# Attention's order found anew, with the strided copy of the first pairs' keys and the landings of late transposing DMAs costed from the trace

## The chip, the core and the metric

The kernel runs on one core of one Trainium2 chip. The metric is device microseconds from start to end of one execution, the median of the runs. In the text PE is TensorE, DVE VectorE, ACT ScalarE, POOL GpSimd and SP SyncE.

## What is computed

An attention with two kinds of keys feeds a mixture of experts. Each query sees the keys less than 16 positions away and, beside them, 24 summaries of blocks of 32 positions (maximum of the keys, mean of the values). The result is the input x of a gate with eight Sinkhorn steps and of eight experts:

```python
k_sum = k.reshape(B, H, nb, block, D).max(axis=3)
v_sum = v.reshape(B, H, nb, block, D).mean(axis=3)
mask_l = np.abs(pos[:, None] - pos[None, :]) < window
scores_l = np.where(mask_l, scale * q @ k.T, -1e9)
scores_s = scale * q @ k_sum.T + np.log(block)
a = softmax(concat([scores_l, scores_s]))
x = a @ concat([v, v_sum])              # 4 batches, 8 heads, 768 positions, 64 wide
P = np.exp(x @ w_gate)                  # x is 3072 x 512, 8 experts
for _ in range(8):
    P /= P.sum(1); P /= P.sum(0); P *= N / E
for e in range(8):                      # w1[e] is 512 x 1024, w2[e] 1024 x 512
    out += P[:, e] * (np.maximum(x @ w1[e], 0) @ w2[e])
```

## The kernel before, in words

**Stages.** The attention handles two heads at once, a *pair*; there are 16, four to a batch. While it runs, PE also does the products of expert 0, in pieces of 384 tokens, as soon as the four pairs of a batch have given their x: the hidden products (L227, tile `hps`, four matmuls for each 128 of the 1,024 hidden rows), their relu (L220), the projection (L237, tile `yps`, two times four matmuls for each 128 tokens) and the copy of that into `out_acc` (L223). From about 116 us on the other seven experts follow, with products of their own kind.

**A pair.** Keys, queries and values are loaded by DMAs that POOL issues. Pairs 0 to 3 are turned on PE (`tr`, `tr_qh`, tiles `tkq`) and copied out with a stride; their queries and all that follows are done in two halves of 384 positions (`pair_half`). Pairs 4 to 11 are turned on PE and copied out contiguously, pairs 12 to 15 by a transposing DMA on SP's queue (`tr_dma`, L358 to L361, `kT` and `qT`); these twelve are handled whole (`pair_whole`). Then come

- `key_max` on DVE (L376 to L385): the block maxima of the keys, into `ksT`;
- the block sums of the values: PE (`vs`, L399) and DVE (`Vs` or `Ve`, L405, and for the whole pairs the copy of L411);
- `near_values` (L415 to L423), for whole pairs: four small DMAs on SP that fetch the neighbouring values into `Ve`. The buffer `Ve` comes free with the second value product of an earlier pair (for pair 11 that is pair 9);
- the scores (L389, `sg`), the scores against the summaries (L489, `ss`), their exponentials on ACT (L514 and its like);
- the masks on DVE (L454) and, for whole pairs, the edges (L462 and L466, twice each);
- the value products on PE (L477 for whole pairs; L537 and L552 for halves), the normalization on DVE (L555 to L567, the last step in L566);
- x turned back, by PE (`tx`, L573) and a copy, or for pairs 10 to 14 by a transposing DMA on SP.

The zeros beside the masked scores of the half pairs are written once for each of the buffers `Eh` (`pads`, L632 to L643).

**What sets the order.** Every engine runs its own instructions strictly in order. That order comes from a list scheduler, `Plan` (L37 to L138), which runs while the kernel is built. The work is cut into units, each added with an engine (or two to choose from), a cost in us, the units that it waits for, the PSUM banks that it opens or uses and a priority; `lag` is the time from the unit's end on its engine until its result may be used. The planner takes, again and again, the unit that could start first on some engine, by priority among those within 0.02 us. The planner's times decide the order and nothing else: on the chip each instruction waits on semaphores for what it needs. Two tables shift its choice: `RANK` adds to the priority of a unit (the key `"S0.14"` is the scores, `S`, part 0, of pair 14), and `ON` pins a unit that two engines could do to one of them. Names in the tables: `k`, `q`, `v`, `w1` loads; `tr`, `kT`, `qT` turning keys and queries and its copy; `km` key maximum; `vs`, `Vs` block sums; `S`, `X` scores and exponential; `mk`, `ed` masks and edges; `ss`, `sx` summary scores; `A`, `no` value products and normalization; `xt`, `x` x turned and copied; `cl` pads; `near` the neighbours; `lg`, `lo` the gate's logits. A bank of the kind `m` holds, in turn, hidden products, projections, and turned keys and queries of the first pairs. When nothing is ready early on, PE is given matmuls that compute nothing (`keep_busy`, L611), so as not to stand idle.

The units that the change touches are added in `pair_start`: the transposing DMAs (L722), and the copies of turned keys (L730, by `tr_out`, L368, on ACT or DVE).

Of the kernel before, what the change touches and what calls it, by code (L numbers as in the profile page):

```python
# [141 lines left out]
def kernel(  # L142
# [21 lines left out]
    PB = H // 2  # L164
# [89 lines left out]
    if True:  # L254
# [19 lines left out]
        add = plan.add  # L274
# [417 lines left out]
        U = {}  # L692
# [22 lines left out]
        def pair_start(i, prio):  # L715
# [4 lines left out]
            for z in range(2 if i >= PB else 1):  # L720
                if i >= 12:
                    U["tr", i, z] = U["kT", i, z] = add("SP", 1.25, lambda z=z: tr_dma(i, z),  # L722
                                                        [U["kq"[z], i]] + (war_k, war_q)[z], prio, lag=5.5)
                    continue
                buf = Buffer(tag)
                U["tr", i, z] = add("PE", 0.5 if i < PB else 0.335, lambda z=z: tr(i, z, tag),
                                    [U["kq"[z], i], U["ident"]] + (war_k, war_q)[z]
                                    + [U["tr", i, 0] if z else U.get(("S", i - 1, 1 if i > PB else 0))],
                                    prio, opens=[buf], shape="col" if i < PB else None)
                U["kT", i, z] = add({"ACT": 0.7, "DVE": 0.475},  # L730
                                    0, lambda z=z: tr_out(U["kT", i, z].on, i, z), [U["tr", i, z]], prio,
                                    uses=[buf])
# [201 lines left out]
        for i in range(4):  # L934
# [1097 lines left out]
```

## Time and profile before

| | |
|---|---|
| median of 3 runs | 658.6 us (656.7 to 659.61) |
| profiled execution | 658.27 us, span of the core 656.6 us |
| mean granted PE clock | 0.998 |
| hidden products of expert 0 (L227), 256 matmuls | 49.3 us of PE, 1.6 us idle before, released by DVE (L223) |
| DMA | 77.73 MB, mean 118 GB/s |
| PE's busy tenths in 40 equal slices | 8 in the first, 9 in nearly all others |

The time of an execution stands 1.67 us above its span in the profile: the span goes from the first to the last instruction that the trace holds. Rows of the timeline read: start in us from the span's start, length in us, engine, line and operation, what is written and read, tile shapes, and a count where several instructions in a row are drawn together; in brackets the idle time of that engine just before, and what ended it. Rows of the stretches read: the stretch and its length, busy time and count of PE, its weight loads, DVE, ACT and POOL, then granted clock, busy share of the DMA engines and GB/s. A PE row's length counts until its last matmul's end, which overlaps the next row's start; the distance of starts tells what PE really spent.

### The profile page before, as it was taken

The numbers are of one execution on the slowest core, as the hardware profiler recorded it, in microseconds if no ns is written. First come the engines' busy times: TensorE is split into PE (matmuls) and PEld (weight loads), VectorE is DVE, ScalarE is ACT, GpSimd is POOL, SyncE is SP. The second block draws the span as 40 slices with busy tenths as digits, with TensorE's granted clock in tenths as the row PEclk, the third lists the DMA queues.
The fourth block names the chain that finished last, engine by engine and source line by source line (L and its number), as shares of the span: only waits on it lengthen the run. The fifth ranks groups of instructions, "written<-read, shape, count | busy, mean of one in ns | idle before, by whom it ended". The sixth has DMA issues, their size and how long they took to land.

```text
span 656.6 us, 15064 instructions
## 1 busy us (share of the span) xinstructions
PE 646.6 (98%) x5569; PEld 446.8 (68%) x5569; DVE 537.5 (82%) x1341; ACT 533.8 (81%) x1210; POOL 255.4 (39%) x320
## 2 busy tenths in 40 slices
PE   8999989999999999999999999999999999999996
PEld 4666656555677676777776767767667777676775
DVE  8889986778889988887799769878889679976866
ACT  6788975666995678898998989899989899898871
POOL 9599504123001022434244243424343326623422
PEclk9999999999999999999999999999999999999999
DMA  9999988400645376987989599978988799987857
GB/s 157 187 152 148 145 92 99 70 1 8 138 112 111 116 124 87 116 110 98 162 107 121 79 157 128 106 96 122 153 106 107 96 168 125 144 139 158 129 69 192
DMA packets 147368, 77.73 MB, mean 118 GB/s; under 512 B 112736, under 2 KB 125280, under 8 KB 147296
## 3 DMA queue, kind: packets, MB, share of 16 engines
q0 software_dynamic: 124864, 62.64, 81.8%
q1 hardware_dynamic: 21472, 13.68, 8.3%
q8 instruction: 43, 0.70, 0.5%
q10 hardware_dynamic: 960, 0.48, 0.3%
q14 instruction: 29, 0.24, 0.1%
HBM read 55.59 MB, written 45.09 MB: 153 GB/s over the span
## 4 chain that ended last, share of the span: by engine, by line
PE 93%; DMA 3%; POOL 2%; DVE 1%; issue 0%; DVEq 0%
PE pab L1086 17%; PE pg L1086 17%; PE py L1092 16%; PE px L1092 13%; PE px L1472 8%; PE hps L227 6%; PE yps L237 6%; PE pab L1144 4%; DMA kT<-kst 1%; DMA qst<-in_q_dram 1%; PE sg L389 1%; PE tkq L355 1%; POOL vx L324 1%; PE av L477 1%; PE ss L489 1%; PE vs L399 1%
## 5 line engine op out<-in xcount | busy, mean ns | idle before, releaser
L1092 PEld LDWEIGHTS <-hf 128*128 128x128 f16 x1840 | 177.5, 98 | 50.0
L1384 POOL DMA_DIRECT2D out_dram<-out_acc x68 | 61.5, 928 | 163.1 <-ACT out_acc L1360 87.9
L1092 PE MATMUL py<-w,hf 128*128 128x256 f16 x656 | 94.8, 273 | 0.0
L1030 DVE TENSOR_TENSOR hf<-hf 128x1024 f16<-128x1024 f16 x142 | 93.0, 689 | 0.0
L1381 POOL DMA_DIRECT2D out_dram<-out_acc x68 | 64.7, 965 | 60.9 <-ACT out_acc L1360 41.0
L1036 DVE CUSTOM_DVE_ANT_0 hf<-pg,c 128x512 f16<-128x512 f32 x84 | 57.8, 688 | 21.5 <-ACT c L1210 14.1
L1360 ACT ACTIVATE out_acc<-py,P_sb 128x256 f32<-128x256 f32 x136 | 62.8, 487 | 7.6 <-PE py L1092 4.1
L1086 PEld LDWEIGHTS <-ws 128*128 128x128 f16 x504 | 46.6, 98 | 30.8 <-issue 0.2
L1086 PEld LDWEIGHTS <-w 128*128 128x128 f16 x520 | 50.0, 99 | 24.9 <-issue 0.4
L203 POOL DMA_DIRECT2D w<-in_moe_w_dram x56 | 45.2, 877 | 53.2 <-PE pg L1086 51.5
L1036 DVE CUSTOM_DVE_ANT_0 hf<-pab,c 128x512 f16<-128x512 f32 x84 | 57.8, 688 | 9.8 <-ACT c L1217 5.7
L1092 PE MATMUL px<-ws,hf 128*128 128x256 f16 x400 | 59.8, 273 | 0.0
L1092 PE MATMUL px<-w,hf 128*128 128x256 f16 x400 | 59.0, 273 | 0.0
L218 ACT ACTIVATE hf<-pg 128x512 f16<-128x512 f32 x84 | 50.9, 606 | 9.8 <-PE pg L1086 9.1
L218 ACT ACTIVATE hf<-pab 128x512 f16<-128x512 f32 x84 | 49.7, 612 | 7.8 <-PE pab L1086 5.7
L1210 ACT COPY c<-pab 128x512 f32<-128x512 f32 x84 | 49.8, 593 | 6.7 <-PE pab L1086 3.7
L1033 DVE TENSOR_TENSOR px<-px,out_acc 128x256 f32<-128x256 f32 x64 | 27.4, 428 | 34.0 <-PE px L1472 33.4
L1217 ACT COPY c<-pg 128x512 f32<-128x512 f32 x84 | 49.7, 592 | 6.3 <-PE pg L1086 5.0
L1086 PE MATMUL pab<-xT,w 128*128 128x512 f16 x184 | 54.4, 379 | 0.0
L1202 ACT COPY pg<-pab 128x512 f32<-128x512 f32 x84 | 49.8, 594 | 3.2 <-PE pab L1144 3.0
L227 PE MATMUL hps<-xT,w 128*128 128x384 f16 x256 | 49.3, 326 | 1.6 <-DVE out_acc L223 1.6
L1086 PE MATMUL pg<-xT,w 128*128 128x512 f16 x168 | 50.0, 379 | 0.0
(191 smaller groups left out, 1536.8 us busy)
## 6 DMA issues: line engine op xcount, KB each, us to landing
out_dram<-out_acc POOLq DMA_DIRECT2D x136, 256.0 KB, 5.0
w<-in_moe_w_dram POOLq DMA_DIRECT2D x8, 1024.0 KB, 11.9
w<-in_moe_w_dram POOLq DMA_DIRECT2D x56, 128.0 KB, 4.6
out_dram<-out_acc SPq DMA_DIRECT2D x28, 256.0 KB, 2.3
vx<-in_v_dram POOLq DMA_DIRECT2D x16, 192.0 KB, 6.0
qst<-in_q_dram POOLq DMA_DIRECT2D x31, 96.0 KB, 5.3
kst<-in_k_dram POOLq DMA_DIRECT2D x24, 96.0 KB, 5.4
out_acc<-out_dram SPq DMA_DIRECT2D x8, 256.0 KB, 4.2
```

Of the source, the lines that this page charges most:

```text
L218: nc.scalar.activation(out=out, in_=in_, func=AF.Relu, bias=0.0, scale=1.0)
L227: nc.tensor.matmul(hp[:, 0:n], lhsT=w1s[e][:, dk, 128 * f:128 * (f + 1)], rhs=xT[:, dk, t0:t0 + n], start=(dk == 0), stop=(dk == KD - 1))
L1030: nc.vector.tensor_tensor(out=out, in0=in0, in1=in1, op=ALU.subtract)
L1036: nc.vector._custom_dve(TENSOR_ADD_SAT, out=out, in0=in0, in1=in1, s0=FLT_MAX, s1=0.0)
L1086: nc.tensor.matmul(bank[:], lhsT=w[:, dk, :], rhs=x[:, dk, :], start=start and dk == 0, stop=dk == KH - 1, skip_group_check=True)
L1092: nc.tensor.matmul(bank, lhsT=a(f)[:, 128 * c:128 * (c + 1)], rhs=w[:, f, :], start=start and f == 0, stop=f == FH - 1, skip_group_check=True)
L1202: nc.scalar.copy(out=B["g" + K][:], in_=B["a" + K][:])
L1210: nc.scalar.copy(out=B["c5" + K][:], in_=B["b" + K][:])
L1360: nc.scalar.activation(out=out_acc[:, (c, HT + c)[t == tb], k * DH:(k + 1) * DH], in_=at(src), func=AF.Copy, scale=scale[:, t, e:e + 1])
L1381: nc.gpsimd.dma_start(out=rows(ta), in_=out_acc[:, c, :], accum_op=ALU.add)
L1384: nc.gpsimd.dma_start(out=rows(tb), in_=out_acc[:, HT + c, :], accum_op=ALU.add)
L1472: nc.tensor.matmul(half(b, k)[:, g, :], lhsT=still2(e, j, g, w, c)[:, i, :], rhs=moving2a(e, g, v)[:, i, :], start=start and g == 0 and i ...
```

## The change

Three costs that the planner is told, and the two tables. The copy of turned keys of pairs 0 to 3 on DVE, which writes with a stride, costs 0.92 us instead of 0.475; a transposing DMA costs SP 1.4 us instead of 1.25; and its result is taken to land 7.5 us after that instead of 5.5, except for pair 15, where it stays 5.5. `RANK` and `ON` are replaced as a whole by tables found for these costs. No instruction is written differently; which engine does a copy, and the order on each engine, follow from the tables and the costs.

```diff
@@ pair_start @@
                 if i >= 12:
-                    U["tr", i, z] = U["kT", i, z] = add("SP", 1.25, lambda z=z: tr_dma(i, z),
-                                                        [U["kq"[z], i]] + (war_k, war_q)[z], prio, lag=5.5)
+                    U["tr", i, z] = U["kT", i, z] = add("SP", 1.4, lambda z=z: tr_dma(i, z),
+                                                        [U["kq"[z], i]] + (war_k, war_q)[z], prio, lag=5.5 if i == 15 else 7.5)
...
-                U["kT", i, z] = add({"ACT": 0.7, "DVE": 0.475},
+                U["kT", i, z] = add({"ACT": 0.7, "DVE": 0.475 if i >= PB else 0.92},
...
         RANK = {
-            "k": -0.92, "k.0": 8.65, "q0": -9.07, "v.0": -5.38, "k.1": -5.25, "q0.1": -4.8, "k.2": 0.79, "q0.2": -0.22, "k.3": 3.33,
...
+            "k": -0.57, "k.0": -5.54, "q0": 6.25, "v": 1.35, "v.0": -0.65, "k.1": 2.88, "q0.2": 6.38, "v.2": 0.34, "v.3": -1.02,
...
         ON = {
-            "q0.0": "DVE", "cl.1": "DVE", "kT0.0": "DVE", "x0.0": "ACT", "qT0.1": "ACT", "x0.1": "ACT", "kT0.2": "ACT", "qT0.2": "ACT",
-            "x0.2": "ACT", "kT1.0": "ACT", "x1.0": "ACT", "kT1.1": "ACT", "x1.1": "DVE", "kT1.2": "DVE", "kT1.3": "ACT", "x1.3": "DVE",
-            "kT0.4": "ACT", "x.4": "DVE", "kT0.5": "ACT", "kT1.5": "ACT", "kT0.6": "ACT", "x.6": "ACT", "kT0.7": "DVE", "kT1.7": "ACT",
-            "x.7": "DVE", "kT0.8": "ACT", "x.8": "ACT", "kT1.9": "DVE", "kT1.11": "ACT", "x.15": "DVE",
+            "cl.1": "ACT", "x0.0": "ACT", "x0.1": "ACT", "kT0.2": "ACT", "qT0.3": "ACT", "x0.3": "ACT", "x1.0": "DVE", "kT1.1": "DVE",
+            "kT1.2": "ACT", "x1.2": "DVE", "kT0.4": "ACT", "kT1.4": "DVE", "x.4": "ACT", "kT0.5": "DVE", "kT1.5": "ACT", "x.5": "ACT",
+            "kT0.6": "ACT", "kT1.6": "DVE", "x.6": "DVE", "kT0.7": "DVE", "x.7": "ACT", "kT1.8": "DVE", "kT0.9": "ACT", "kT0.10": "DVE",
+            "kT1.10": "ACT", "kT0.11": "ACT", "x.15": "ACT",
         }
```

What the changed tables give, read off the built instruction orders: on PE 11,114 rows (matmuls and weight loads) instead of 11,116, one idle matmul of 19 left out, and the last 8,185 in one order in both programs; DVE 1,251 instructions instead of 1,259, ACT 1,129 instead of 1,132, with the last 886 and the last 968 in the same order; POOL's order unchanged. Engines change for some copies: the pads of the second `Eh` buffer go from DVE to ACT, ahead of the copy of pair 0's first queries; two strided key copies go from DVE to ACT, while DVE gets more of the contiguous copies; three relus of expert 0 go from DVE to ACT. The scores of the last pairs stood on PE in the order 11, 12, 13, 14, 15 and stand as 12, 11, 14, 13, 15. On SP, of the DMAs for the late pairs (`near` is four of them):

```
before: kT12 near10 qT12 kT13 qT13 kT14 near11 qT14 near12 x10 kT15 qT15
after:  kT12 qT12 near10 kT13 qT13 near11 kT14 qT14 near12 x10 kT15 qT15
```

On DVE, the order around pair 14's key maximum becomes: normalization of pair 10, a copy of yps, masks of pair 12, block sums of pair 12, edges of pair 12, first mask of pair 11, key maximum of pair 14, second mask and edges of pair 11, key maximum of pair 13, normalization of pair 11.

90 rows, old and new, of the table RANK are left out of this document.

## The prediction

> **What bounds the kernel now.** I read the page first, for the share of each engine, then the stretches, to see where PE is not full.
>
> ```profile
> span 656.6 us, 15064 instructions
> PE 646.6 (98%) x5569; PEld 446.8 (68%) x5569; DVE 537.5 (82%) x1341; ACT 533.8 (81%) x1210; POOL 255.4 (39%) x320
> ...
> PE 93%; DMA 3%; POOL 2%; DVE 1%; issue 0%; DVEq 0%
> ```
>
> PE has 93% of the chain that ended last: only time in which PE waits, or does matmuls that compute nothing, can be won. The stretches (span, then busy time of PE first) place it.
>
> ```profile
> 82.00:92.00 10.00, 8.42 (x91) 5.18 (x90) 7.61 (x24) 6.94 (x15) 0.35 (x2) 1.00 1.33 124
> ...
> 300.00:400.00 100.00, 100.00 (x837) 71.89 (x836) 80.63 (x174) 89.50 (x220) 38.71 (x46) 1.00 0.91 124
> ```
>
> The expert stage at 300 us has no idle PE, and the last 8,185 of PE's 11,114 rows stand in one order in both programs: that stage only starts earlier or later. The attention stage, 0 to about 116 us, decides. Busy time flatters it, since a pipelined matmul counts until its end, so I read starts. Here is PE in the worst stretch (start, length, and in brackets its idle time).
>
> ```profile
> 83.53 0.81 PE L227 MATMUL hps<-xT,w 128*128 128x384 f16 x4
> 85.91 0.81 PE L227 MATMUL hps<-xT,w 128*128 128x384 f16 x4 [1.57 <-DVE out_acc L223]
> ...
> 86.74 2.28 PE L227 MATMUL hps<-xT,w 128*128 128x384 f16 x12
> 88.86 0.35 PE L477 MATMUL av<-vx,em 128*128 128x65 bf16 x6
> ...
> 89.57 0.32 PE L489 MATMUL ss<-qT,ksT 128*128 128x384 bf16 x1
> 89.73 1.46 PE L227 MATMUL hps<-xT,w 128*128 128x384 f16 x8
> 91.13 0.59 PE L389 MATMUL sg<-qT,kT 64*128 64x160 bf16 x12
> ```
>
> Eight hidden matmuls of L227 take 1.46 us, four 0.81: 0.162 apiece and 0.16 for the last one's end. Four should thus hand over after 0.65, but the next four start 2.38 after them: 1.73 lost. The twelve at 86.74 need 1.94 and hold PE for 2.12: 0.18 more. Together 1.9 us. DVE names the cause.
>
> ```profile
> 81.25 0.56 DVE L566 TENSOR_TENSOR xs<-av,rc 128x384 f16<-128x384 f32 x1
> 84.00 0.36 DVE L381 TENSOR_TENSOR kh<-kT 128x384 bf16<-128x384 bf16 x1 [2.19 <-DMA kT<-kst]
> ...
> 85.18 0.68 DVE L223 COPY out_acc<-yps 128x512 f32<-128x512 f32 x1
> 85.78 0.55 DVE L454 TENSOR_TENSOR em<-er,band 128x768 bf16<-128x768 bf16 x1
> 86.24 0.28 DVE L405 TENSOR_TENSOR Ve<-vs,own 64x128 bf16<-64x128 f32 x1
> ...
> 86.97 0.54 DVE L220 TENSOR_SCALAR h<-hps 128x384 f16<-128x384 f32 x1
> ...
> 87.98 0.19 DVE L462 TENSOR_TENSOR Ee<-er,band 32x80 bf16<-32x80 bf16 x1
> ...
> 88.85 1.03 DVE L454 TENSOR_TENSOR em<-er,band 128x768 bf16<-128x768 bf16 x2
> ```
>
> The key maximum of pair 14 stood at DVE's head, waited 2.19 us for its transposing DMA, and the copy of yps behind it freed PE's bank late. SP's rows of that stretch:
>
> ```profile
> 74.61 2.00 SPq L360 DMA_TRANSPOSE kT<-kst  x1
> 76.72 0.59 SPq L420 DMA_DIRECT2D Ve<-vx  x1
> ...
> 79.41 1.27 SPq L360 DMA_TRANSPOSE qT<-qst  x1
> ```
>
> From issue to landing, the transposing DMAs of L360 as the view of that line has it, and the small copies into Ve as the DMA view has it (number, KB, median):
>
> ```profile
> DMA to landing us min/median/max: 2.7/8.3/9.4
> ```
>
> ```profile
> Ve<-vx SPq DMA_DIRECT2D x48, 10.2 KB, 4.6
> ```
>
> A planner that gives the transposing ones 6.75 us (1.25 and a lag of 5.5), where the median is 8.3, makes that mistake.
>
> **The change part by part.** The three costs are read by the planner alone; what runs differs by order and by engine of evacuation. POOL's queue keeps its order, so the loads stay; PE drops one idle matmul of 19.
>
> *The stretch at 83 us, won.* In the new order the copy of yps follows pair 10's normalization on DVE directly, and pair 14's key maximum stands behind that copy (0.60), both masks of pair 12 (1.03), its block sums (0.73), its edges (0.87) and one mask of pair 11 (0.46): 3.7 us of DVE work after 81.8, so about 85.5. The PE wait of 1.9 us goes: **minus 1.9**. Nothing excludes less; if pair 14's keys came 2 us later still, the masks and edges of pair 11 would wait behind them and the gain would be spent.
>
> *The first 34 us, lost.* Rows first:
>
> ```profile
> 4.69 1.31 ACT L643 COPY Eh<-zeros 128x224 bf16<-128x224 bf16 x3
> 6.08 0.48 ACT L223 COPY qT<-tkq 128x384 bf16<-128x384 bf16 x1
> 9.56 0.94 DVE L223 COPY kT<-tkq 128x768 bf16<-128x768 bf16 x1
> 19.56 0.36 PE L339 MATMUL tkq<-ident,qst 128*64 128x128 bf16 x6 [0.31 <-DMA qst<-in_q_dram]
> 21.43 0.55 DVE L223 COPY qT<-tkq 128x384 bf16<-128x384 bf16 x1
> 22.38 1.01 ACT L514 ACTIVATE erh<-sg 128x992 bf16<-128x992 f32 x1
> 24.65 0.65 PE L537 MATMUL av<-vx,Eh 128*128 128x65 bf16 x16
> 26.55 0.65 PE L537 MATMUL av<-vx,Eh 128*128 128x65 bf16 x16
> 33.03 1.03 PE L237 MATMUL yps<-w,h 128*128 128x512 f16 x4
> ...
> 34.16 0.59 PE L389 MATMUL sg<-qT,kT 64*128 64x160 bf16 x12
> 34.68 0.34 PE L573 MATMUL tx<-ident,xs 128*128 128x128 f16 x3
> ```
>
> The pads of Eh1 move from DVE to ACT and stand ahead of pair 0's query copy: 1.31 us more there, a copy at 7.3 instead of 6.08, first scores 0.7 late. Two strided key copies (0.94 each) leave DVE in return. Both orders then meet at 19.56, where PE waits for a query load that POOL issues as before: until there the change costs **nothing**; the cover is this wait, and without it the 0.7 would count.
>
> From there I count along the new order. Pair 0's second scores now precede pair 1's query copy on DVE (0.55, done at 22.0); on ACT the exponential (1.01) and a query copy precede the fourth x, which frees the first hidden matmuls at about 23.3. Seven hidden matmuls, a score group (0.4) and five more bring the first value product of the second half to 25.7, against 24.65. The new order has by then done that score group, which the old one does later. On to pair 4's scores: four value products (2.6, from rows 24.65 and 26.55 with what lies between), 20 hidden matmuls (3.25), four groups of transposes of x, two of k and q, scores and summaries, about 2.2: 33.75. The old order reaches them at 34.16 with four more yps matmuls (0.87 to the next start) and a summary (0.16) done, 1.03 in all, and one transpose group (0.17) open: like for like 33.3. **Plus 0.45**; bounds minus 0.3 (the score group hidden) and plus 1.2 (what the first exponentials slip).
>
> *The new wait.* Pair 14's scores now stand ahead of pair 13's on PE. PE would reach them at 91.13 (pair 13's scores now), plus 0.52 for pair 14's own, minus 2.63 for what comes between (0.52; 88.86 to 89.57, 0.71; 89.73 to 91.13, 1.40), minus 1.9, plus 0.45: 87.6. Their queries come by the DMA issued at 79.41. On SP the four copies for pair 11 (from 76.72, 2.7 us with all four) move ahead of pair 14's keys; pair 9's second value product, whose end they need, is done some 1.6 us earlier, so I put the copies at 74.0, the keys at 76.5 instead of 74.61, and the queries at 78.4. With 8.3 to 9.4 they land at 86.7 to 87.8; if the engines, not the issue, set the landing, at the old 87.7 to 88.8. PE waits 0 to 1.2, and everything behind it on PE too, since no row passes the head. I take **plus 0.4**, the middle of the nearer half. The keys, at 84.8 to 85.9, meet DVE at 85.5; its 2.5 us up to pair 11's edges end at 88.0 to 88.4, beside the same PE wait.
>
> [...]
>
> Sum: minus 1.9, plus 0.45, plus 0.4 is **minus 1.05**. On the profiled execution, 658.27 us with a span of 656.6, that is a span of 655.5 and a time of 657.2. The median of the three runs is 658.6, 0.3 above, and they spread from 656.7 to 659.6; I put **657.3**.
>
> **The rivals.** *Slower: PE blocks on pair 14's queries.* If the copies for pair 11 go out only at 76.72, as now, keys follow at 79.4, queries at 81.4, and with 9.4 they land at 90.8: a wait of 3.2, a sum of plus 1.8, 660.1. It decides from a landing at 89.0 on. For it: the in-order PE and the issue of 2.00 at 74.61, where SP itself was held. Against: those copies are free to start earlier. *Everything won:* the queries are in time and the first 34 us cost nothing, with 0.3 won there: minus 2.2 and up to 0.25 of smaller waits, 655.9. For it: landings no longer underpriced. *The fix doesn't hold:* keys late, the wait moves from the copy of yps to pair 11's edges; minus 1.9 becomes nothing, sum 0 to plus 0.9: 658.7. For it: the keys are issued 1.9 us later than now.
>
> **How the numbers follow.** Forecast 0.46, everything won 0.22, doesn't hold 0.14, slower 0.18: the new wait sits where a landing that no row shows meets an engine that lets nothing pass, so its bad side weighs more than its distance says. About 0.5% (3.3 us) is what a measurement of this kernel can tell from no change: faster means below 655.3, slower above 661.9. The forecast lies inside, and so does all but the ends of its bounds with 1 us of scatter around. Faster: half of "everything won", 0.11, and the lower end of the forecast, 0.03: 0.14. Slower: a bit over half of "blocks", which with the upper bound of the first 34 us (0.75 more) and scatter passes 661.9: 0.10. Same: 0.76. The range runs from 654.4 (everything won, with 1.5 of gains and scatter below it) to 661.0 (blocked, with the 0.75 and little more), about 1 in 10 left out on either side.
>
> **What would show it.** Right: no DVE wait over 0.5 us on kT between 80 and 90, the eight L227 matmuls there in 1.46, first hidden matmul at about 23.3, pair 14's scores at 87.5 to 88.2. Wrong: a gap on PE ahead of L389 near 88, or first scores and first hidden matmuls at their old times. A change of PE's idle time behind 120 us would contradict the whole argument.

## The result, and the profile after

| | before | changed |
|---|---|---|
| median (range) of 22 runs each, side by side | 659.29 us (656.26 to 661.27) | 657.25 us (655.99 to 659.04) |
| ratio, 95% interval | | 0.9974 [0.9963, 0.9986] |
| profiled execution: time, span | 658.27, 656.6 | 656.57, 654.5 |

The change makes the kernel 2.0 us faster, 0.3%, clear of noise but below the half per cent that was called the same; 657.3 had been forecast. Two later comparisons gave less: 657.19 against 658.30, 0.9984 [0.9969, 0.9999], and 657.19 against 657.67, 0.9989 [0.9973, 1.0004], which is not clear of noise by itself. One execution of the changed kernel took 1128.71 us at a granted clock of 0.565; it is left out of all figures and traces here.

The two profiled executions are 1.70 apart in time and 2.1 in span, since the time of the changed one stands 2.07 above its span instead of 1.67.

The kernel before also scatters more: over all comparisons the middle eight in ten of its 106 runs lie between 656.8 and 660.4, of the changed kernel's 45 between 656.8 and 658.0. The fast ends are equal; what the changed kernel lacks is the upper end.

The head of the page of the changed kernel: PE's share of the chain goes from 93% to 96%, DMA's from 3% to 1%.

```profile
span 654.5 us, 15071 instructions
PE 645.5 (99%) x5568; PEld 446.2 (68%) x5568; DVE 536.7 (82%) x1339; ACT 533.6 (82%) x1212; POOL 256.4 (39%) x320
...
PE 96%; POOL 2%; DMA 1%; DVE 0%; ACT 0%; issue 0%; DVEq 0%
```

The bad stretch, 8.42 of 10 us busy before, is full (same columns as before):

```profile
82.00:92.00 10.00, 10.00 (x116) 6.34 (x114) 9.37 (x33) 9.20 (x18) 0.47 (x2) 1.00 1.31 131
```

PE there: twenty hidden matmuls in one piece, 3.34 from their start to the next (20 by 0.162 is 3.24), then pair 14's scores with hardly a wait, and the eight L227 matmuls of 88.62 hand over after 1.39.

```profile
84.03 3.41 PE L227 MATMUL hps<-xT,w 128*128 128x384 f16 x20
87.37 0.59 PE L389 MATMUL sg<-qT,kT 64*128 64x160 bf16 x12
87.89 0.36 PE L477 MATMUL av<-vx,em 128*128 128x65 bf16 x6
...
88.62 1.46 PE L227 MATMUL hps<-xT,w 128*128 128x384 f16 x8
90.01 0.59 PE L389 MATMUL sg<-qT,kT 64*128 64x160 bf16 x12
...
90.73 0.34 PE L483 MATMUL av<-Ve,Ee 128*128 128x130 bf16 x3
```

The last of these rows is pair 12's value product with its neighbours, which will matter below. DVE does the copy of yps at 81.22 and comes to pair 14's keys without waiting:

```profile
81.22 0.68 DVE L223 COPY out_acc<-yps 128x512 f32<-128x512 f32 x1
...
84.42 0.56 DVE L454 TENSOR_TENSOR em<-er,band 128x768 bf16<-128x768 bf16 x1
84.89 0.35 DVE L381 TENSOR_TENSOR kh<-kT 128x384 bf16<-128x384 bf16 x1
```

For pair 14 on SP, issue first, then the time to landing as the view of L360 gives it for the keys alone: 75.86 and 8.8, so they landed at 84.65, 0.24 ahead of DVE. The queries, issued at 78.01, landed at 86.67, 0.70 ahead of PE.

```profile
75.86 1.98 SPq L360 DMA_TRANSPOSE kT<-kst  x1
78.01 1.50 SPq L360 DMA_TRANSPOSE qT<-qst  x1
```

```profile
DMA to landing us min/median/max: 8.8/8.8/8.8
```

**Where PE lost time, in every trace.** The orders differ, so single rows can't be compared. From some point (134 to 140 us) PE's order is the same in all kernels; I call this the common part. I charged each matmul ahead of it the mean distance of starts of its line and shape (the upper tenth cut off), the idle matmuls nothing, and call what is left loss. The same work, 121.05 us, comes out for all. It is my working, good to about 0.1; one trace each, in us. The kernels are those of the next section.

| trace | to 38 us | 38 to 83 | 83 to 92 | behind 92 | common part starts |
|---|---|---|---|---|---|
| before | 11.46 | 1.19 | 2.30 | 0.34 | 136.34 |
| before, 2nd | 11.34 | 1.18 | 2.24 | 0.34 | 136.13 |
| before, 3rd | 11.19 | 1.17 | 1.49 | 0.35 | 135.25 |
| changed | 11.69 | 1.30 | 0.33 | 0.18 | 134.56 |
| changed, 2nd | 11.33 | 1.32 | 0.33 | 0.18 | 134.20 |
| before, key maximum late | 11.67 | 1.63 | 0.98 | 0.71 | 136.04 |
| the same, 2nd | 12.04 | 1.08 | 1.73 | 0.34 | 136.24 |
| changed, key maximum early | 11.38 | 1.31 | 5.06 | 0.46 | 139.25 |
| changed, copies for 11 late | 12.38 | 1.20 | 0.42 | 2.23 | 137.28 |
| changed, queries of 14 late | 11.14 | 1.31 | 1.24 | 0.19 | 134.92 |
| changed, pads on DVE | 10.91 | 1.54 | 0.33 | 0.18 | 134.01 |
| before, new landing | 11.20 | 0.98 | 1.61 | 4.97 | 139.81 |
| changed, old DMA costs | 11.42 | 1.13 | 0.50 | 4.34 | 138.44 |

So the first pair of traces has PE 1.78 ahead at the common part: minus 1.97 between 83 and 92, minus 0.16 behind, plus 0.23 and 0.11 ahead of it. The last group of matmuls, L1092 in before and in the changed kernel,

```profile
650.29 1.04 PE L1092 MATMUL py<-w,hf 128*128 128x256 f16 x8
```

```profile
648.25 1.04 PE L1092 MATMUL py<-w,hf 128*128 128x256 f16 x8
```

is 2.04 apart; the other 0.26 comes at one place of the expert stage (last section).

### The profile page after: what moved, and what is told of

The parts are those of the page before. It is cut to its first block, busy times and chain, and to the rows that moved or that the text cites. A ratio compares the mean times of both kernels' runs of the same rounds, so it can differ in the third digit from the quotient of the medians.

```text
span 654.5 us, 15071 instructions
## 1 busy us (share of the span) xinstructions
PE 645.5 (99%) x5568; PEld 446.2 (68%) x5568; DVE 536.7 (82%) x1339; ACT 533.6 (82%) x1212; POOL 256.4 (39%) x320
## 4 chain that ended last, share of the span: by engine, by line
PE 96%; POOL 2%; DMA 1%; DVE 0%; ACT 0%; issue 0%; DVEq 0%
PE pab L1086 17%; PE pg L1086 17%; PE py L1092 16%; PE px L1092 13%; PE px L1472 8%; PE hps L227 6%; PE yps L237 6%; PE pab L1144 4%; DMA qst<-in_q_dram 1%; PE sg L389 1%; PE tkq L355 1%; PE av L477 1%; PE ss L489 1%; POOL vx L324 1%; PE vs L399 1%; PE av L483 1%
## 5 line engine op out<-in xcount | busy, mean ns | idle before, releaser
L1092 PEld LDWEIGHTS <-hf 128*128 128x128 f16 x1840 | 177.5, 98 | 50.0
L1384 POOL DMA_DIRECT2D out_dram<-out_acc x68 | 61.7, 931 | 162.3 <-ACT out_acc L1360 87.8
L1092 PE MATMUL py<-w,hf 128*128 128x256 f16 x656 | 94.8, 273 | 0.0
L1092 PE MATMUL px<-ws,hf 128*128 128x256 f16 x400 | 59.8, 273 | 0.0
L1092 PE MATMUL px<-w,hf 128*128 128x256 f16 x400 | 59.0, 273 | 0.0
L1086 PE MATMUL pg<-xTs,ws 128*128 128x512 f16 x168 | 50.0, 379 | 0.0
```

Of the source, the lines that this page charges most:

```text
L1086: nc.tensor.matmul(bank[:], lhsT=w[:, dk, :], rhs=x[:, dk, :], start=start and dk == 0, stop=dk == KH - 1, skip_group_check=True)
L1092: nc.tensor.matmul(bank, lhsT=a(f)[:, 128 * c:128 * (c + 1)], rhs=w[:, f, :], start=start and f == 0, stop=f == FH - 1, skip_group_check=True)
L1384: nc.gpsimd.dma_start(out=rows(tb), in_=out_acc[:, HT + c, :], accum_op=ALU.add)
```

## The experiments

The theory: the change wins what PE lost behind DVE's wait for pair 14's keys. Rivals: the score order and the engines of the copies bring it; or the wait only hands over to another one. The kernels that move one unit keep the planner's order and hold that unit back, or bring it forward, when the instructions are written out; nothing else moves. Where the changed kernel did not run beside a kernel, the distance to it is taken to the 657.25 of the first comparison; the ratio to before, measured side by side, is the surer figure.

### Before, with pair 14's key maximum behind the second mask of pair 11

```diff
-        course = plan.order()
+        course, late = plan.order(), {U["km", 14]: U["mk", 11, 1]}
...
-            if u.fn is not None:
-                u.fn()
+            for x in [] if u in late else [u] + [x for x in late if late[x] is u]:
+                x.fn is not None and x.fn()
```

> The kernel before with one move: the key maximum of pair 14 (four DVE instructions) stands behind the second mask of pair 11 instead of ahead of the copy of yps; tables, costs, engines and all other orders are those of before. Theory (the gain of the change is the DVE wait on a late transposing DMA, which held back the copy of yps): no DVE wait over 0.3 us on kT near 84, the eight L227 matmuls at 83.5 in 1.46, PE's 1.9 us gone, and the 0.26 at 92 perhaps with it; median 1.9 to 2.2 below before, as the changed kernel or a little better, since the first 34 us aren't touched. Rival (the gain comes from the new score order and the other engines of the copies; a queue of DVE work that is full anyway hands the wait to the next unit): PE's idle time moves to the relu or the edges behind, median within 0.7 of before.

Measured: 657.64 against 658.66, 0.9983 [0.9971, 0.9996]. Half of what was expected. The wait is gone, but PE gives 0.9 back between 89 and 95; there DVE waited for pair 10's x:

```profile
92.68 0.56 DVE L566 TENSOR_TENSOR xs<-av,rc 128x384 f16<-128x384 f32 x1 [1.01 <-DMA xT<-xs]
```

This trace is of the longest of the twelve runs, so the kernel was run again beside the changed one.

> The kernel before with pair 14's key maximum behind the second mask of pair 11, a second time, for its trace: the first was taken in its slowest run of twelve, 2.1 us above its median, and there PE gave 0.9 of the 1.9 won back between 89 and 95, where DVE waited 1.0 for the landing of pair 10's x at 92.6. If that was the late landing of this one execution, the trace now shows the 1.9 won and at most 0.4 given back, and the ratio to the changed kernel on the same chip is 1.000 plus or minus 0.001. If the old order of scores and edges gives it back in every execution, 0.5 to 0.9 us are lost between 89 and 95 again, and the median stays 0.4 to 0.9 above the changed kernel's.

Measured: 658.12 against 657.67 for before, 0.9993 [0.9977, 1.001], and 657.19 for the changed kernel on that chip. By the medians it is the second case: 0.93 above the changed kernel, though this trace, too, is of the longest of its runs (659.37). What gives the gain back is another wait than in the first trace. DVE no longer waits for keys (its 0.69 ahead of the copy of yps is for PE), the hidden matmuls run in 1.46, and then PE stands 0.92 ahead of pair 12's value product, for the copies of its neighbours:

```profile
83.15 0.69 DVE L223 COPY out_acc<-yps 128x512 f32<-128x512 f32 x1 [0.69 <-PE yps L237]
...
85.88 0.35 DVE L381 TENSOR_TENSOR kh<-kT 128x384 bf16<-128x384 bf16 x1
```

```profile
84.08 1.46 PE L227 MATMUL hps<-xT,w 128*128 128x384 f16 x8
...
91.99 0.35 PE L483 MATMUL av<-Ve,Ee 128*128 128x130 bf16 x3 [0.92 <-DMA Ve<-vx]
```

So the theory's size falls: of the 1.9, the first comparison kept 1.0 and the second no gain clear of noise. Before has a further wait close behind, and while PE stands in the first, that one runs out unseen.

### Before, two more traces

> A second trace of the kernel before. The times of before spread over 5 us, those of the changed kernel over 3. Theory: the part of the spread that the changed kernel lacks is the landing of pair 14's keys, at which DVE and, through the copy of yps, PE wait; so PE's loss at 83 to 86 here is 1.9 us plus the difference of that landing against PE's own position to the first trace (the keys landed at 83.98, PE reached the place at 84.2), and every us of later landing is a us of time. Rival: the spread comes from the end of the program (the last store) or the loads of the first 22 us, and PE loses 1.9 here again, whatever the time.

> A third trace of the kernel before, with the same expectations: by the theory PE's loss at 83 to 86 follows the landing of pair 14's keys; by the rival it is 1.9 in every trace and the spread is in the first 22 us and behind PE's last matmul.

Measured: 658.21 and 657.68 us. The second trace repeats the first: DVE waits 2.15 for the keys (landed at 83.78), PE 1.52.

```profile
83.80 0.36 DVE L381 TENSOR_TENSOR kh<-kT 128x384 bf16<-128x384 bf16 x1 [2.15 <-DMA kT<-kst]
```

```profile
85.71 0.81 PE L227 MATMUL hps<-xT,w 128*128 128x384 f16 x4 [1.52 <-DVE out_acc L223]
```

In the third, nature made the first experiment: the keys landed at 81.75, DVE waited 0.26, PE lost nothing at 83 to 86, and then 1.20 at pair 12's neighbours:

```profile
81.77 0.36 DVE L381 TENSOR_TENSOR kh<-kT 128x384 bf16<-128x384 bf16 x1 [0.26 <-DMA kT<-kst]
```

```profile
90.99 0.35 PE L483 MATMUL av<-Ve,Ee 128*128 128x130 bf16 x3 [1.20 <-DMA Ve<-vx]
```

PE's loss at 83 to 86 does follow the landing, but its loss from 83 to 92 falls only from 2.30 to 1.49, for landings 2.2 us apart. "Every us of later landing is a us of time" is wrong. That this accounts for the whole scatter of before isn't shown: its longest run (662.3) has no trace.

Why are pair 12's copies late? The fourth of them was issued here at 83.80, the moment at which the first copy for pair 11, eight SP DMAs ahead of it, landed (83.78):

```profile
83.80 0.58 SPq L422 DMA_DIRECT2D Ve<-vx  x1
```

In the first trace it was the third, at 84.00, when pair 14's keys, eight ahead, landed (83.98). In the new SP order pair 12's copies stand eight behind pair 13's DMAs and the copies for pair 11, landed by 80.9; they go out at 80.00 to 82.68, land by 89.18, and PE asks at 90.7.

The late issue is not all of it. In the first trace of before the fourth copy went out later still, at 84.62, and landed at 89.22. What tells these traces apart is a single packet of the instruction queue (q8 in the DMA view, 0.02 MB; the times are those of the trace's DMA packets). Between 80 and 104 us, in all traces here, no DMA of SP landed from 0.6 us behind the start of such a packet until 0.8 us behind its end. In the third trace one was moved from 88.48 to 90.05: the third copy landed at 88.59, the fourth at 90.95. In the trace of b_km14_again it came from 90.18 to 91.12, the third copy landed at 89.98 and the fourth at 91.94; in that of b_km14_late from 90.72 to 91.78; the fourth copy got in at 90.83, and pair 10's x landed at 92.58. In the changed kernel it began at 90.10, and 89.39 in the second trace, when the copies and that x had landed. The keys of pair 14 fit too: 83.98 and 83.78 are 1.27 and 1.38 behind the end of an earlier packet (82.71 and 82.40), and 81.75, in the third trace, is 0.18 behind the start of one (81.57 to 82.57). No run moves such a packet, so that it holds the landings back is not shown.

### Changed, with the key maximum ahead of the copy of yps

The converse: `ahead = {U["yo", 768, 1]: U["km", 14]}` in the same loop, and the unit is written out ahead of that copy.

> The changed kernel with one move, the reverse: the key maximum of pair 14 stands ahead of the copy of yps (behind pair 10's normalization), as in before. Theory: DVE waits from 81.2 to the landing at 84.7, 3.4 us; DVE has no idle time from 80 to 93, so everything behind is later by that, the copy of yps at 85.9 and the edges of pair 11 at about 90.9; PE loses 2.5 to 3.4 us, median 659.8 to 660.6. Rival (only the bank of the copy of yps counts, as in before): plus 1.9, 659.2. Second rival (the order of DVE near 82 is not what moved the time): within 0.7 of the changed kernel's 657.25.

Measured: 662.70, 1.0054 [1.0034, 1.0073] to before, 5.4 above the changed kernel. That is more than any of the theories said. DVE's wait of 3.21 was expected. But it wasn't the bank of yps that held PE: it was that of pair 12's block sums, which DVE empties still later.

```profile
84.20 0.36 DVE L381 TENSOR_TENSOR kh<-kT 128x384 bf16<-128x384 bf16 x1 [3.21 <-DMA kT<-kst]
...
86.91 0.28 DVE L405 TENSOR_TENSOR Ve<-vs,own 64x128 bf16<-64x128 f32 x1
```

```profile
87.24 0.48 PE L489 MATMUL ss<-qT,ksT 128*128 128x384 bf16 x1 [3.52 <-DVE Ve L405]
87.52 4.62 PE L227 MATMUL hps<-xT,w 128*128 128x384 f16 x20
```

And the twenty hidden matmuls took 4.62 instead of 3.41. The column before the last two of the stretches is the granted clock: 0.50 behind the wait, 1.00 only from 90 us on.

```profile
87.00:88.00 1.00, 0.76 (x3) 0.40 (x3) 0.94 (x4) 0.00 (x0) 0.00 (x0) 0.50 0.74 136
90.00:91.00 1.00, 1.00 (x8) 0.59 (x6) 0.89 (x5) 0.78 (x3) 0.06 (x1) 1.00 0.00 0
```

So 5.06 of loss is 3.5 of waiting, and 1.2 of the rest is these twenty matmuls at the lower clock.

### Changed, with the copies for pair 11 behind pair 14's DMAs on SP

In the loop of the first experiment: `late = {U["near", 11]: U["kT", 14, 1]}`.

> The changed kernel with the four small copies for pair 11 on SP behind pair 14's two transposing DMAs instead of ahead of them. If SP's DMAs land one after the other in the order of issue, with the backlog setting the time: pair 14's keys land 2 to 2.7 us earlier (82.0 to 82.7 instead of 84.65), its queries at 84 to 84.7 instead of 86.67, the copies at 85 to 86.7 instead of 80.2 to 81.6. If the load on the engines sets it: keys and queries land within 0.7 of now. Either way the time stays within 0.4 of 657.25 by the theory (the queries had 0.7 to spare, the value products of pair 11 need the copies at 87.9); a gain over 0.5 would say that pair 14's landings still cost PE something that the trace of the changed kernel doesn't show.

Measured: 659.30, 1.0003 [0.9991, 1.0016] to before, 2.1 above the changed kernel. Neither alternative expected it. The keys, issued 1.38 earlier, landed at 84.28, 0.37 earlier; the queries at 87.60, 0.93 later. The third row below is the fourth copy for pair 12: it stands eight behind pair 14's queries and goes out at 87.61. Behind it, pair 15's keys go out at 89.72 instead of 84.80.

```profile
74.48 1.59 SPq L360 DMA_TRANSPOSE kT<-kst  x1
78.51 1.23 SPq L360 DMA_TRANSPOSE qT<-qst  x1
...
87.61 0.58 SPq L422 DMA_DIRECT2D Ve<-vx  x1
...
89.72 1.22 SPq L360 DMA_TRANSPOSE kT<-kst  x1
```

They land at 93.44; their key maximum stands at DVE's head, and PE waits for a bank behind it. It is the wait of before, one pair later:

```profile
93.47 0.36 DVE L381 TENSOR_TENSOR kh<-kT 128x384 bf16<-128x384 bf16 x1 [2.12 <-DMA kT<-kst]
```

```profile
95.48 0.34 PE L489 MATMUL ss<-qT,ksT 128*128 128x384 bf16 x1 [1.87 <-DVE xs L566]
```

### The changed kernel again, and with pair 14's queries late

> The changed kernel unaltered, as the control beside the other kernels of this call: ratio to the kernel before 0.996 to 0.999. Its second trace shows how far landings and waits differ between two executions: by the theory pair 14's keys land at 84 to 85 with no DVE wait over 0.5, and the first hidden matmul (22.65 in the first trace) may differ by some tenths, since what stands ahead of it waits for loads.

Measured: 657.19, 0.9984 [0.9969, 0.9999].

> The changed kernel unaltered, for a second trace at full clock and as the control beside the next kernel. Expected: no PE wait over 0.3 between 80 and 95, pair 14's keys at 84 to 85, the first hidden matmul at 22.0 to 22.7, ratio to before 0.997 to 0.999.

Measured: 657.19, 0.9989 [0.9973, 1.0004]; keys at 84.19, first hidden matmul at 22.51, no PE wait from 80 to 95, as expected. This is the second trace of the changed kernel.

Beside the former of the two ran the changed kernel with `late = {U["kT", 14, 1]: U["near", 12]}`:

> The changed kernel with pair 14's query DMA on SP behind the four copies for pair 12 (issue at about 81.5 instead of 78.0). It prices the rival that the prediction feared: pair 14's scores stand ahead of pair 13's on PE, reached at 87.4, and nothing passes them. By that the queries land at 88.6 to 89.2, PE waits 1.2 to 1.8 ahead of L389, and the median is 1.2 to 2 above the changed kernel. If landings near 88 come in one bunch however they were issued (the POOL loads of before last until 88.6), the queries land within 0.7 of 86.7 and the time stays within 0.4. If PE has other slack behind (the edges of pair 12 and 11 come no sooner), half of it: plus 0.6 to 0.9.

Measured: 657.55, 0.9984 [0.9968, 1.0]: 0.4 above the control, inside the scatter. The queries go out 4.68 later and land 1.02 later (87.69), since they now take 5.0 instead of 8.7; PE waits 0.83 and no more.

```profile
82.69 1.22 SPq L360 DMA_TRANSPOSE qT<-qst  x1
```

```profile
87.73 0.59 PE L389 MATMUL sg<-qT,kT 64*128 64x160 bf16 x12 [0.83 <-DMA qT<-qst]
```

That is nearest to the second alternative (near 88 landings come together, however the DMAs were issued), though the landing moved by more than its 0.7.

### Changed, with the pads of the second Eh buffer on DVE

```diff
+            u.on = "DVE" if u is U["cl", 1] else u.on
```

> The changed kernel with the pads of the second Eh buffer back on DVE, all else in the changed order. Theory (until the query load that PE awaits near 20 us nothing ahead of it counts): the first scores are up to 0.4 earlier, the first hidden matmul at 22.65 moves by less than 0.2, and the median stays within 0.3 of 657.25. Rival (the pads on ACT are what the first 34 us lost): first hidden matmul near 22.1, stall left after it unchanged, median lower by 0.3 to 0.6.

Measured: 657.68, 0.9987 [0.9974, 1.0] to before. First scores at 7.17 instead of 7.55, first hidden matmul at 22.09 instead of 22.65, and no gain in the time. The 22.09 is what the rival named, but the rows ahead of it side with the theory. The query load that PE awaits went out at 11.49 here and at 11.51 and 11.48 in the two traces of the changed kernel; it landed at 18.79, 19.35 and 19.21, and the first hidden matmul followed 3.30 later in all three. So the load moved, and not the work behind the pads. Its landing is at least part of why the loss to 38 us is 10.91 here, the lowest of all. In the time, 0.3 or less can't be told.

### The new landing alone, and the new tables with the old DMA costs

Before's tables with the new landing (`lag=5.5 if i == 15 else 7.5`), and the new tables with the old costs of the transposing DMAs (1.25 and 5.5); the strided cost stays with its tables.

> The kernel before with the new landing of transposing DMAs alone (lag 7.5, pair 15's 5.5), with the old tables and the other two old costs. In its order the copy of yps stands between the two normalizations of pair 10, ahead of pair 14's key maximum, and pair 13's key maximum, too, stands later; the score order 11, 12, 13, 14, 15 is kept. Theory (it is the planner's belief of the landing, not the tables, that took the wait out): no DVE wait over 1 us on kT near 84, median 1 to 2 below before, at or near the changed kernel. Rival (the new tables bring the gain): within 0.5 of before.

> The changed kernel with the old costs of transposing DMAs (1.25, lag 5.5) under its new tables and the new strided cost. In its order the copy of yps stands ahead of pair 13's and 14's key maxima, but pair 13's stands ahead of both normalizations of pair 10, and pair 15's queries ahead of its keys on SP. Theory: what counts is which key maximum stands ahead of a copy that PE waits for; here none of pair 14 does, so most of the gain stays, but pair 13's (landing 78.3) and 14's come earlier than the landings: DVE waits of 0.5 to 1.5 us, median 0.3 to 1.2 above the changed kernel. Rival (tables alone carry the gain): within 0.3 of the changed kernel. Rival (costs carry it): at before's median or above.

Measured: 662.28, 1.0056 [1.0036, 1.0076] to before, and 661.69, 1.0044 [1.0028, 1.0059]. Both are slower than either kernel: each of these parts of the change is worse than nothing. (The 1.4 of SP and the 0.92 of the strided copy weren't run by themselves.) The first still has DVE wait at 83 (1.37), which costs PE 0.89, and the planner, from there on another order, makes a new wait at 102, where DVE's edges come behind a piece of expert 0's work:

```profile
102.34 0.63 PE L483 MATMUL av<-Ve,Ee 128*128 128x130 bf16 x3 [2.90 <-DVE Ee L462]
```

```profile
103.00:104.00 1.00, 1.00 (x16) 0.75 (x15) 0.00 (x0) 0.43 (x1) 0.00 (x0) 0.50 0.00 0
```

The second has none at 83, as the theory had it, but three smaller ones at 100 to 106, and the clock again:

```profile
100.79 0.50 PE L399 MATMUL vs<-vx,m_blk 128*128 128x128 bf16 x6 [1.13 <-ACT er L441]
102.01 0.34 PE L477 MATMUL av<-vx,em 128*128 128x65 bf16 x6 [0.71 <-DVE Ve L405]
...
102.36 2.65 PE L227 MATMUL hps<-xT,w 128*128 128x384 f16 x8
```

Eight hidden matmuls in 2.65 instead of 1.46. What the theory said of these two rested on the one stretch at 83 us; what a planner's other order does 20 us later can't be read from that. That the second lies above before, as the rival "costs carry it" has it, says no more: its loss is at 100 us, not at 83.

## Why the prediction was right, and where it wasn't

- **The stretch at 83 us, minus 1.9.** Right in place and size: minus 1.97 between 83 and 92. That DVE's wait for the keys is what held PE there is shown by before without it (PE's wait at 83 is gone), by the third trace of before, whose keys came early, and by the converse (5.06 of loss once the key maximum stands ahead, though by another bank). But the reason given is incomplete, and against the third trace of before the stretch gives minus 1.16. The prediction knew one wait; there was a second behind it, which removing the first alone uncovers: pair 12's neighbour copies (0.92 and 1.20), or, in the trace of b_km14_late, pair 10's x. So about half of the gain came in, or less. In the two traces of the changed kernel these copies had landed 1.5 and 1.9 ahead of PE. Its SP order sends them out earlier, which fits, but no run moved these copies alone, and the order of the scores changed too. The prediction counted the landings of keys and queries on SP and not those of the copies for pair 12.
- **The first 34 us, plus 0.45.** Too large, if it exists. The first scores came 0.39 late (0.7 forecast), the first hidden matmul at 22.65 (23.3 forecast), pair 4's scores at 33.53 (33.75 forecast, like for like 33.3 in before). The loss to 38 us is 11.69 and 11.33 against 11.46, 11.34 and 11.19: 0.2 more on the mean, within what unchanged programs scatter. The cover, the wait for a load near 20 us, held.

```profile
22.65 1.30 PE L227 MATMUL hps<-xT,w 128*128 128x384 f16 x7
...
33.53 0.59 PE L389 MATMUL sg<-qT,kT 64*128 64x160 bf16 x12
```

- **The new wait, plus 0.4.** Nothing. PE came at 87.37 (87.6 forecast), the queries went out at 78.01 (78.4) and landed at 86.67 (86.7 to 87.8): the issue was estimated well, and the lower end of the landing was the true one. The other end, a wait of up to 1.2, had the queries land where they did in before (88.32); they landed 1.65 earlier. The median of 8.3 for the transposing DMAs and the 4.6 for the copies into Ve, which the prediction shows together, don't compare like with like: in before these copies took from 1.9 to 7.8, and beside pair 14's keys (9.4) and queries (8.9) the six small copies issued from 76.72 to 81.42 took 7.4 to 7.8.
- **The rival "blocks".** Its price was much too high: 3.2 of wait for an issue at 81.4. Issued at 82.69, the queries cost 0.83. The step that failed is that issue plus 9.4 gives the landing.
- **"The fix doesn't hold"** describes, with another transfer, the kernel before with only the key maximum moved: 657.64 and 658.12. For the changed kernel it didn't come about.
- **The sum.** Minus 1.05 was forecast, minus 1.78 measured up to the common part and minus 2.04 at PE's last group. The two costs were about 0.2 and 0.4 too high, and 0.26 came at 247 us, where the prediction had said that any change of PE's idle time would contradict it; as a hitch at one place it leaves the argument on the first 140 us as it was. That the forecast time hits the median within 0.1 us is luck: it was worked out from 658.3, before's median over 22 runs is 659.3, and the 1.0 by which the start was too low is the 1.0 by which the gain was too small.

## What to carry to other kernels

A wait that PE shows may cover the next one (here one of 1.9 covered one of 0.92 or 1.20): before pricing its removal, look for what PE would ask for next and when that lands. A DMA's landing is read from the traffic around it, not from its issue plus a mean: pair 14's queries took 8.7 issued at 78.01 and 5.0 issued at 82.69. An instruction that needs it belongs behind everything on its engine that frees a bank for PE; with pair 14's key maximum ahead of the copy of yps, the changed kernel took 5.4 us more. Costs and priority tables of a planner belong together: the two parts that were tried alone lost 3 to 4 us here.

## What the hardware showed that was not expected

**Landings come in a bunch.** SP's DMAs issued from 75.86 to 84.80 in the changed kernel landed from 84.65 to 89.87, in order; the first took 8.8, the last 5.1. POOL's last load of the attention, in flight at the same time, took 12.6 and landed at 88.6:

```profile
75.98 1.02 POOL L324 DMA_DIRECT2D vx<-in_v_dram  x1
```

```profile
DMA to landing us min/median/max: 12.6/12.6/12.6
```

A transposing DMA issued near its end, at 87.29, took 3.3, and the small copies issued behind it, up to 100 us, 1.9 to 3.6. Queries that go out 4.68 later and land 1.02 later (a_qT14_late) agree with the bunch. What makes it, no run tells. Nor is it shown whether the packets of the instruction queue above have a part: one was moved from 81.30 to 82.25 here, and between 81.64 and 84.65 nothing of SP's landed.

**SP had at most eight DMAs under way.** In nine places of these traces a copy goes out 0.02 after the landing of the one eight ahead of it (84.00 behind 83.98, 83.80 behind 83.78, 87.61 behind 87.60 among them), and of 1,261 DMAs on SP with eight ahead of them none goes out before that landing. They use eight semaphores in turn; whether the chip or the built program sets the eight, no run tells. In these traces what stood eight behind a slow transfer waited for its landing.

**PE's clock.** Waits of 1.57 us (before) and 1.87 (a_near11_late) left the granted clock at 1.00. With one of 2.90 (b_lag), with one of 3.52 (a_km14_early), and with 1.13 and 0.71 close together (a_oldsplag, PE busy 0.50 of the 2 us from 100 to 102) it fell to 0.50 and was back at 1.00 after about 3.4 us: an estimate from stretches of 1 us, in a_km14_early 0.77, 0.50, 0.50 and 0.52 from 86 to 90 us, that is 0.46, 1, 1 and 0.96 us at 0.50 if the rest was at 1.00. What decides whether it falls, no run tells.

**A fixed 0.26.** The five traces with before's PE order have a hitch of 0.26 in the expert stage at one place, here four matmuls of L1092 that hand over after 0.64 instead of 0.44,

```profile
247.10 0.60 PE L1092 MATMUL px<-ws,hf 128*128 128x256 f16 x4
247.74 0.59 PE L1086 MATMUL pg<-xT,w 128*128 128x512 f16 x2
```

and none of the eight traces with another order has it there (two of them, a_pads_dve and a_oldsplag, have one of 0.31 at 557 and 561 us):

```profile
245.32 0.60 PE L1092 MATMUL px<-ws,hf 128*128 128x256 f16 x4
245.76 0.59 PE L1086 MATMUL pg<-xT,w 128*128 128x512 f16 x2
```

No engine is named as waited for; its cause stays open.
